# Two units that take turns, weights in three groups of blocks, and a plain first product in the last layers

## The chip, the cores and the metric

The kernel runs on one core of a Trainium2 chip. Five engines of the core work beside each other, each through its own queue in order: TensorE (PE, matmuls; its weight loads are PEld), VectorE (DVE), ScalarE (ACT), GpSimd (POOL) and SyncE (SP, which issues DMAs). The metric is the device time of one execution in microseconds; lower is better.

## The reference

Attention feeds a layer of eight experts, and that feeds one dense feed-forward layer. For 2 batches of 576 tokens, 8 heads of 64:

```
scores = q k^T / 8 + min(-(cum_i - cum_j), 0), causal;  attn = softmax(scores) v
x      = attn as 1152 tokens x 512
P      = exp(x w_gate - max), then 8 rounds of row and column normalisation
out    = sum over e of P[:, e] * (relu(x w1[e]) w2[e])       # w1: 512x1024, w2: 1024x512, 8 experts
y      = softplus(out w_in) w_out                            # w_in: 512x2048, w_out: 2048x512
```

All of it is float32; the last layer's weights come as 64-bit floats and are turned into float32 on the chip.

## The kernel before

Attention takes the first 118 us. After it the program runs 20 layers of one shape, numbered x = 0 to 19: each takes a 512x512 piece of a first weight and a 512x512 piece of a second one. Layers 0 to 15 are the experts' (NX = 16, two per expert; XE = 2 is the first layer of the second expert), layers 16 to 19 the dense layer's. Tokens are kept in two groups g of 576, each in two halves of 288 columns (HB).

Each float32 operand is held as two float32r parts, high and low, and a product is three matmuls: high by high, high by low, low by high.

The first product of a layer, x times w1, is done in Strassen's way with seven block products in place of eight. A `Unit` (x, p, g) makes two of the four 128-row blocks of the hidden layer, by the methods p1, p2, p6, p7, p5, p3, p4 in that order; each is six matmuls of 288 columns. p = 0 is unit a, p = 1 unit b, so that "a6" is p6 of unit a. The units share partial results within a PSUM bank: p1 leaves its product in bank `self.a`, ACT copies it out as `v` (L232, method `copy`), p6 adds its own product onto the same bank, ACT copies that as `u`, p5 adds again, and so on. So p6 may not start until the copy v is done, nor p5 until u is. DVE adds the copies to the other products (L245, L263, L274).

`evict` turns a finished block into the second product's operand `hh` (high) and `hl` (low). In layers 0 to 15 this is a ReLU: ACT L184, DVE L185. In layers 16 to 19 it is a softplus: ACT takes abs, exp and ln (L191 to L193), DVE L197 and L198, POOL L199 and L200 (which writes hh), DVE L203 and L204 (which writes hl). `defer` puts such pieces off by some flushes, and `flush` runs at each product and at each quarter of a second product.

`downs` is the second product: for each of nine tiles of 128 tokens, four quarters ("d") of three matmuls of 512 columns, in two PSUM banks y1 and y2 that alternate; DVE then adds the sum to `acc` (L296, L299).

The weights are prepared one layer ahead. `prep1` splits a w1 piece of one unit and makes four sums of its blocks: ACT L124 and DVE L128 for three raw blocks at once, POOL L125, L126, L129, L130 for the sums, then ACT L134 and DVE L136 for the four sums at once. `prep2` does the second weight (ACT L147, DVE and POOL L150). `convert` turns the 64-bit weights into float32 (L783 to L799, 32 pieces) from layer 2 on; `gate_steps` works out P during layers 0 and 1; `turn` transposes the experts' output for the dense layer; `build` makes the Strassen sums of x.

The order of all this is written by hand, as strings: `play` takes one product or one "d" after the other, and after each "d" the function `quarter` moves the background generators (`back`, `gates`, `conv`) on by one step. Within a layer the strings are, for the second group of tokens and then for the next layer's first group:

```
play("a1 a2", u) ... play("a6 a7 a5", u)
play("b1 d b2 d a3 d a4 d", u, d)              # then prep1(x + 1, 0) starts
play("b6 d b7 d b5 d d b3 d b4 d d d d d d d", u, d)
play("d d d d", {}, d)                         # prep1(x + 1, 1) has just started
play("a1 d a2 d a6 d d a7 d a5 d", u, d)
play("b1 d b2 d a3 d a4 d b6 d b7 d b5 d d b3 d b4 d", u, d)
```

Of the kernel before, what the change touches and what calls it, by code (L numbers as in the profile page):

```python
# [20 lines left out]
def attention_moe_ffn(ctx, tc, q, k, v, s, w_gate, w1, w2, w_in, w_out, out):  # L21
# [40 lines left out]
    A11, A12, A22, S1, S2, S3, S4 = range(7)  # L62
# [4 lines left out]
    def build(g, c, xr, xt_pool, quick):  # L67

        sub = nc.vector if quick else nc.gpsimd
        h, l = xh[g], xl[g]  # L70
        x1, x2 = xr[:, c, :], xr[:, c + 2, :]
        o = h[:, B11, c, :]
        nc.scalar.activation(out=o, in_=x1[:, :HB], func=AF.Copy)
        nc.vector.tensor_tensor(out=l[:, B11, c, :], in0=x1[:, :HB], in1=f(o), op=ALU.subtract)
        yield
        xt = xt_pool.tile([P, 4, HB], F32, tag="xt", name="xt", bufs=1)
        sub.tensor_tensor(out=xt[:, 0, :], in0=x1[:, HB:], in1=x1[:, :HB], op=ALU.subtract)
        yield
        o = h[:, B21:B22 + 1, c, :]
        z = x2.rearrange("p (j n) -> p j n", j=2)  # L80
        nc.scalar.activation(out=o, in_=z, func=AF.Copy)
        nc.gpsimd.tensor_tensor(out=xt[:, 2, :], in0=x2[:, HB:], in1=x1[:, HB:], op=ALU.subtract)
        sub.tensor_tensor(out=xt[:, 1, :], in0=x2[:, HB:], in1=xt[:, 0, :], op=ALU.subtract)
        yield
        nc.vector.tensor_tensor(out=l[:, B21:B22 + 1, c, :], in0=z, in1=f(o), op=ALU.subtract)
        sub.tensor_tensor(out=xt[:, 3, :], in0=x2[:, :HB], in1=xt[:, 1, :], op=ALU.subtract)
        yield
        o = h[:, T1:T4 + 1, c, :]
        nc.scalar.activation(out=o, in_=xt, func=AF.Copy)
        yield  # L90
        nc.vector.tensor_tensor(out=l[:, T1:T4 + 1, c, :], in0=xt, in1=f(o), op=ALU.subtract)
        yield
# [8 lines left out]
    order = [(x, which, i) for x in range(NH) for which in (1, 2) for i in range(2)]  # L101
    nxt = [0]

    def load_next():
        if nxt[0] >= len(order):
            return
        x, which, i = key = order[nxt[0]]
        nxt[0] += 1
        t = raw_p.tile([P, WQ], F32, tag="raw", name="raw")
        src = (w1 if which == 1 else w2)[x, i] if x < NX else wd[which][(x - NX) * 2 + i]  # L110
        nc.sync.dma_start(out=t, in_=src)
        raw_t[key] = t

    def prep1(x, p):

        if x >= NH:
            return
        t = raw_t.pop((x, 1, p))
        hi = w_p.tile([P, 7, HW], F32R, tag="w1h", name="w1h")
        lo = w_p.tile([P, 7, HW], F32R, tag="w1l", name="w1l")  # L120
        s4 = ws_p.tile([P, 4, HW], F32, tag="ws", name="ws")
        wt[(x, 1, p)] = (hi, lo)
        t = t.rearrange("p (b n) -> p b n", b=4)
        nc.scalar.activation(out=hi[:, :S1], in_=t[:, 1:], func=AF.Copy)  # L124
        nc.gpsimd.tensor_tensor(out=s4[:, 0, :], in0=t[:, 0, :], in1=t[:, 3, :], op=ALU.add)  # L125
        nc.gpsimd.tensor_tensor(out=s4[:, 1, :], in0=s4[:, 0, :], in1=t[:, 1, :], op=ALU.subtract)  # L126
        yield
        nc.vector.tensor_tensor(out=lo[:, :S1], in0=t[:, 1:], in1=f(hi[:, :S1]), op=ALU.subtract)  # L128
        nc.gpsimd.tensor_tensor(out=s4[:, 2, :], in0=t[:, 1, :], in1=t[:, 0, :], op=ALU.subtract)  # L129
        nc.gpsimd.tensor_tensor(out=s4[:, 3, :], in0=t[:, 2, :], in1=s4[:, 1, :], op=ALU.subtract)  # L130
        load_next()
        yield
        yield
        nc.scalar.activation(out=hi[:, S1:], in_=s4, func=AF.Copy)  # L134
        yield
        nc.vector.tensor_tensor(out=lo[:, S1:], in0=s4, in1=f(hi[:, S1:]), op=ALU.subtract)  # L136
        yield

    def prep2(x, i):
        if x >= NH:  # L140
            return
        t = raw_t.pop((x, 2, i))
        hi = w2_p[0].tile([P, 2, DM], F32R, tag=f"w2h{i}", name=f"w2h{i}", bufs=1)
        lo = w2_p[0].tile([P, 2, DM], F32R, tag=f"w2l{i}", name=f"w2l{i}", bufs=1)
        wt[(x, 2, i)] = (hi, lo)
        t = t.rearrange("p (c n) -> p c n", c=2)
        nc.scalar.activation(out=hi, in_=t, func=AF.Copy)  # L147
        yield
        for c in range(2):
            (nc.gpsimd if i else nc.vector).tensor_tensor(out=lo[:, c], in0=t[:, c], in1=f(hi[:, c]), op=ALU.subtract)  # L150
        load_next()
        yield
# [25 lines left out]
    lag = [0, 1]  # L178

    def evict(x, z, q, cols):  # L180

        hh, hl = hb[0][:, q, cols], hb[1][:, q, cols]
        if x < NX:
            nc.scalar.activation(out=hh, in_=z, func=AF.Relu)  # L184
            nc.vector.scalar_tensor_tensor(out=hl, in0=z, scalar=0.0, in1=f(hh), op0=ALU.max, op1=ALU.subtract)  # L185
# [9 lines left out]
        def sums():  # L195

            nc.vector.tensor_scalar(a2, a1, 1.0, -1.0, ALU.add, ALU.add)  # L197
# [797 lines left out]
```

## Time and profile before

| | |
|---|---|
| median of 3 runs | 1245.52 us (1243.07 to 1245.73) |
| the profiled execution | 1244.63 us, its span 1242.9 us |
| busy share of the span | PE 90%, PEld 78%, DVE 68%, ACT 42%, POOL 36% |
| instructions | 17931 |

The profiled execution's time is 1.7 us above its span, which counts from the first to the last instruction. A busy PE isn't PE at its peak: matmuls overlap, and what one costs is read from the distance of two starts. The idle time behind a row, in brackets, names what ended it.

### The profile page before, as it was taken

To read this page: it belongs to the slowest core of one execution; us is meant where nothing else is said; L and a number is where in the kernel's file an instruction comes from. 1 tells how busy PE (TensorE), PEld (TensorE's weight loads), DVE (VectorE), ACT (ScalarE), POOL (GpSimd) and SP (SyncE) were. 2 spreads that over 40 slices of the span, in tenths; PEclk is the share of its full clock that TensorE was granted. 3 is DMA by queue.
4 is the path that set the end of the run, shared out by engine and by line. 5 is a ranking of instruction groups with operands and counts; after the bars stand their busy time and mean duration, and the time that the engine had idled before them with its cause. 6 is when DMAs were issued, how large, how long until landed. Compare 5 with 4: busy or idle time off the path is not lost.

```text
span 1242.9 us, 17931 instructions
## 1 busy us (share of the span) xinstructions
PE 1113.2 (90%) x6596; PEld 963.3 (78%) x6596; DVE 850.4 (68%) x1703; ACT 520.4 (42%) x1138; POOL 450.4 (36%) x529
## 2 busy tenths in 40 slices
PE   6998998998999999999999999999999488796867
PEld 4766987888788888888888888898897467675766
DVE  4554437476878878778787787854556866676763
ACT  5987433232333433334334233332344545434441
POOL 8884102022432223323232232320212555546451
PEclk9989999899999999999999999999999789898999
DMA  5310101021322223222222132110110000101001
GB/s 172 99 59 14 52 17 51 17 96 58 119 85 86 82 75 107 86 85 94 76 95 101 69 102 80 66 60 17 69 51 17 35 18 17 51 18 38 14 9 68
DMA packets 30424, 78.48 MB, mean 63 GB/s; under 512 B 6048, under 2 KB 10656, under 8 KB 30336
## 3 DMA queue, kind: packets, MB, share of 16 engines
q1 hardware_dynamic: 27768, 68.93, 16.3%
q0 software_dynamic: 2560, 8.39, 1.7%
q8 instruction: 52, 0.85, 0.3%
q14 instruction: 36, 0.29, 0.1%
q10 hardware_dynamic: 8, 0.01, 0.0%
HBM read 66.02 MB, written 10.82 MB: 62 GB/s over the span
## 4 chain that ended last, share of the span: by engine, by line
PE 42%; DVE 28%; POOL 10%; ACT 9%; issue 9%; DMA 1%; SPq 1%; DVEq 0%; POOLq 0%; ACTq 0%
PE py L289 19%; PE ph L224 17%; DVE hl L185 3%; ACT hh L184 3%; DVE a L203 2%; DVE hl L204 2%; DVE acc L299 2%; DVE w2l L150 2%; POOL hh L200 2%; PE sc L462 2%; DVE ph L274 1%; DVE w1l L136 1%; DVE a L198 1%; POOL a L199 1%; POOL cm L798 1%
## 5 line engine op out<-in xcount | busy, mean ns | idle before, releaser
L224 PE MATMUL ph<-xh,w1h 128*128 128x288 f32 x1120 | 344.3, 307 | 89.5 <-ACT u L232 44.5
L224 PE MATMUL ph<-xh,w1l 128*128 128x288 f32 x1120 | 337.2, 301 | 0.0
L224 PE MATMUL ph<-xl,w1h 128*128 128x288 f32 x1120 | 336.7, 301 | 0.0
L224 PEld LDWEIGHTS ph<-xh,w1h 128*128 128x128 f32 x1120 | 216.2, 193 | 126.1 <-ACT u L232 52.5
L289 PE MATMUL py<-w2h,hh 128*128 128x512 f32 x720 | 292.2, 406 | 11.7 <-DVE acc L296 9.4
L289 PE MATMUL py<-w2h,hl 128*128 128x512 f32 x720 | 291.1, 404 | 1.2 <-DVE hl L204 1.2
L289 PE MATMUL py<-w2l,hh 128*128 128x512 f32 x720 | 291.2, 404 | 0.0
L224 PEld LDWEIGHTS ph<-xl,w1h 128*128 128x128 f32 x1120 | 217.2, 194 | 18.7
L224 PEld LDWEIGHTS ph<-xh,w1l 128*128 128x128 f32 x1120 | 217.0, 194 | 0.0
L798 POOL TENSOR_TENSOR cm<-cm,ct 128x512 f32<-128x512 f32 x32 | 42.4, 1324 | 365.4 <-DVE ct L797 365.4
L184 ACT ACTIVATE hh<-ph 128x288 fp32r<-128x288 f32 x192 | 78.3, 409 | 218.6 <-DVE ph L274 112.2
L289 PEld LDWEIGHTS py<-w2h,hl 128*128 128x128 f32 x720 | 138.7, 193 | 35.3 <-DVE hl L204 1.6
L289 PEld LDWEIGHTS py<-w2h,hh 128*128 128x128 f32 x720 | 140.2, 195 | 28.1 <-POOL a L199 10.6
L289 PEld LDWEIGHTS py<-w2l,hh 128*128 128x128 f32 x720 | 139.8, 194 | 13.3
L185 DVE SCALAR_TENSOR_TENSOR hl<-ph,hh 128x288 fp32r<-128x288 f32 x192 | 86.8, 455 | 62.0 <-ACT hh L184 60.2
L232 ACT ACTIVATE u<-ph 128x288 f32<-128x288 f32 x160 | 65.3, 408 | 141.7 <-PE ph L224 141.5
L299 DVE SCALAR_TENSOR_TENSOR acc<-py,gate,acc 128x512 f32<-128x512 f32 x126 | 93.6, 743 | 36.5 <-PE py L289 36.5
L150 POOL TENSOR_TENSOR w2l<-raw,w2h 128x512 fp32r<-128x512 f32 x40 | 53.1, 1347 | 165.6 <-ACT w2h L147 165.4
L199 POOL TENSOR_TENSOR a<-a,a 128x288 f32<-128x288 f32 x64 | 52.0, 813 | 108.2 <-DVE a L197 108.2
L134 ACT ACTIVATE w1h<-ws 128x1024 fp32r<-128x1024 f32 x40 | 42.1, 1051 | 73.1 <-POOL ws L130 73.1
L185 DVE SCALAR_TENSOR_TENSOR hl<-t,hh 128x288 fp32r<-128x288 f32 x64 | 43.3, 677 | 32.7 <-ACT hh L184 32.7
L203 DVE TENSOR_TENSOR a<-a,hh 128x288 f32<-128x288 f32 x64 | 38.4, 601 | 39.7 <-POOL hh L200 39.7
(177 smaller groups left out, 1598.6 us busy)
## 6 DMA issues: line engine op xcount, KB each, us to landing
raw<-in_w SPq DMA_DIRECT2D x64, 512.0 KB
f<-in_w_in SPq DMA_DIRECT2D x16, 512.0 KB
f<-in_w_out SPq DMA_DIRECT2D x16, 512.0 KB
wd<-cm POOLq DMA_DIRECT2D x32, 256.0 KB, 2.7
raw<-wd SPq DMA_DIRECT2D x16, 512.0 KB
out<-acc SPq DMA_DIRECT2D x9, 256.0 KB
vv<-in_v SPq DMA_DIRECT2D x8, 256.0 KB
qk<-in_k SPq DMA_DIRECT2D x7, 288.0 KB
```

Source lines behind the costliest of these rows:

```text
L134: nc.scalar.activation(out=hi[:, S1:], in_=s4, func=AF.Copy)
L150: (nc.gpsimd if i else nc.vector).tensor_tensor(out=lo[:, c], in0=t[:, c], in1=f(hi[:, c]), op=ALU.subtract)
L184: nc.scalar.activation(out=hh, in_=z, func=AF.Relu)
L185: nc.vector.scalar_tensor_tensor(out=hl, in0=z, scalar=0.0, in1=f(hh), op0=ALU.max, op1=ALU.subtract)
L199: nc.gpsimd.tensor_tensor(out=a2, in0=a1, in1=a2, op=ALU.subtract)
L200: nc.gpsimd.tensor_tensor(out=hh, in0=a3, in1=a2, op=ALU.add)
L203: nc.vector.tensor_tensor(out=a3, in0=a3, in1=f(hh), op=ALU.subtract)
L224: nc.tensor.matmul(o, u, v, start=(start and c == 0 and n == 0), stop=(c == 1 and n == 2), skip_group_check=True)
L232: nc.scalar.activation(out=t, in_=self.a, func=AF.Copy)
L289: nc.tensor.matmul(py, u, v, start=(k == 0 and n == 0), stop=(k == NF - 1 and n == 2))
L299: nc.vector.scalar_tensor_tensor(out=a, in0=py, scalar=gate_t[0][:, t, e:e + 1], in1=a, op0=ALU.mult, op1=ALU.add)
L798: nc.gpsimd.tensor_tensor(out=m, in0=m, in1=f(t), op=ALU.add)
```

## The change

It has these parts.

1. The two units take turns product by product: "a1 b1 a2 b2 a6 b6 ..." in place of five products of a, then two of b and so on. The strings are new (`A_SEQ`, `B_SEQ`), and the first group's products of layer 0 run ahead of the loop.
2. A w1 piece's seven blocks lie in three groups of 2, 2 and 3 blocks with tiles of their own, in place of one tile. `prep1` takes a group (0, 1, 2) for both units, and starts where the last product that reads the old group is past: "=0", "=1", "=2" in the strings. The four sums are made in place, in the raw tile, in two generators; a split is one group of ACT and DVE steps.
3. The second weight is prepared in quarters (`prep2(x, ft)`, "w0" to "w3") at the end of the layer before, in place of halves at the layer's start.
4. In layers 16 to 19 the first product is plain (`plain`): eight products of twelve matmuls for each group of tokens, no copies, no DVE adds. `turn` writes hh and hl of x directly, without `build`.
5. `evict` is put off in smaller pieces; in the softplus the second sum goes from POOL to DVE, and the high part is an ACT copy.
6. `downs` takes tiles 0 and 1, and 7 and 8, in pairs; a flush and a background step (`step`) follow each product and each quarter. The gate moves every sixth step, the conversion every third one and in seven steps a piece in place of four.

```
-        hi = w_p.tile([P, 7, HW], F32R, tag="w1h", name="w1h")
-        lo = w_p.tile([P, 7, HW], F32R, tag="w1l", name="w1l")
...
+        nb = (2, 2, 3)[g]
+        hi = w_p.tile([P, nb, HW], F32R, tag=f"w1h{g}", name=f"w1h{g}")
+        lo = w_p.tile([P, nb, HW], F32R, tag=f"w1l{g}", name=f"w1l{g}")
+        wt[x, 1, p, g] = (hi, lo)
+        for o, src in parts:
+            nc.scalar.activation(out=hi[:, o], in_=t[:, src], func=AF.Copy)
+            yield
+            yield
+            nc.vector.tensor_tensor(out=lo[:, o], in0=t[:, src], in1=f(hi[:, o]), op=ALU.subtract)
+            yield
...
             nc.vector.tensor_scalar(a2, a1, 1.0, -1.0, ALU.add, ALU.add)
+            nc.gpsimd.tensor_tensor(out=a2, in0=a1, in1=a2, op=ALU.subtract)
             nc.vector.scalar_tensor_tensor(out=a3, in0=z, scalar=0.0, in1=a3, op0=ALU.max, op1=ALU.add)
-            nc.gpsimd.tensor_tensor(out=a2, in0=a1, in1=a2, op=ALU.subtract)
-            nc.gpsimd.tensor_tensor(out=hh, in0=a3, in1=a2, op=ALU.add)
+
+        def high():
+            nc.vector.tensor_tensor(out=a3, in0=a3, in1=a2, op=ALU.add)
+            nc.scalar.activation(out=hh, in_=a3, func=AF.Copy)
 
         def rest_():
-            nc.vector.tensor_tensor(out=a3, in0=a3, in1=f(hh), op=ALU.subtract)
-            nc.vector.tensor_tensor(out=hl, in0=a3, in1=a2, op=ALU.add)
-
-        defer(lag[0], sums)
-        defer(lag[1], rest_)
+            nc.vector.tensor_tensor(out=hl, in0=a3, in1=f(hh), op=ALU.subtract)
+
+        defer(0, sums)
+        defer(2, high)
+        defer(3, rest_)
...
+    def plain(x, p, g, i, j):
+
+        o = ps.tile([P, 512], F32, tag="sc", name="ph", bufs=4)[:, :HB]
+        wh, wl = wt[x, 1, p, i]
+        ops = []
+        for r in range(2):
+            for c in range(2):
+                k = slice(c * P, (c + 1) * P)
+                h, l = xh[g][:, 2 * r + c, j, :], xl[g][:, 2 * r + c, j, :]
+                ops += [(wh[:, r, k], h), (wh[:, r, k], l), (wl[:, r, k], h)]
+        for n, (u, v) in enumerate(ops):
+            nc.tensor.matmul(o, u, v, start=(n == 0), stop=(n == 11))
+            if n == 5:
+                flush()
+                yield
+        flush()
+        evict(x, 0, o, p + 2 * i, slice(g * S + j * HB, g * S + (j + 1) * HB))
+        yield
...
+        A_SEQ = "a1 b1 a2 b2 =0 d d a6 d d b6 d d a7 d d b7 =1 d a5 d b5 d a3 d b3 d a4 d b4 d d"
+        B_SEQ = ("d d =2 a1 d d b1 d a2 d b2 d a6 d b6 d a7 d b7 d a5 d b5 d d w0 a3 d d w2 b3 d d w1 a4 d d w3 b4")
+        A_PLAIN = "p p p p d d p d p d p d p d =0 p d p d p d p d p d p d p d p =1 d d d"
+        B_PLAIN = "d d =2 d d p p d p d p d p p d p d p d p d p d p d d w0 p d d w2 p d d w1 p d d w3 p p"
+        A_GROUPS = [(0, 1), (2,), (3,)]
+        B_GROUPS = [(4,), (5,), (6,), (7, 8)]
```

How the order of the instructions moves, at two places. The first is ACT where the next layer's first products begin, in a layer that also converts weights: u and v are the copies that p6 and p5 wait for, w1h the split weights, cm the conversion. Before:

```order
L784 ACTIVATE cm<-f_5314 128x512
L124 ACTIVATE w1h<-raw 128x768
L134 ACTIVATE w1h<-ws 128x1024
L232 ACTIVATE v_5580<-ph 128x288
L184 ACTIVATE hh<-ph 128x288
L232 ACTIVATE u_5608<-ph 128x288
```

And in the change:

```order
L294 ACTIVATE v<-ph 128x288
L145 ACTIVATE w1h_5253<-raw_4813 128x256
L294 ACTIVATE v<-ph 128x288
L145 ACTIVATE w1h_5253<-raw_4813 128x512
L234 ACTIVATE hh<-ph 128x288
L145 ACTIVATE w1h_5298<-raw_4865 128x256
L871 ACTIVATE cm<-f_5128 128x512
L234 ACTIVATE hh<-ph 128x288
L294 ACTIVATE u<-ph 128x288
```

The copies v of both units now stand ahead of the weights' pieces, which are smaller, and three other instructions at most stand between a copy and the next one.

The second place is DVE in one of the layers 16 to 19; hl is the low part that ends an eviction, acc the sum of a second product. Before:

```order
L197 TENSOR_SCALAR a_11103<-a_11102 128x288
L198 SCALAR_TENSOR_TENSOR a_11104<-ph,a_11104 128x288
L197 TENSOR_SCALAR a_11125<-a_11124 128x288
L198 SCALAR_TENSOR_TENSOR a_11126<-ph,a_11126 128x288
L274 TENSOR_TENSOR ph<-ph,u_11033 128x288
L203 TENSOR_TENSOR a_11104<-a_11104,hh 128x288
L204 TENSOR_TENSOR hl<-a_11104,a_11103 128x288
L203 TENSOR_TENSOR a_11126<-a_11126,hh 128x288
L204 TENSOR_TENSOR hl<-a_11126,a_11125 128x288
```

And in the change:

```order
L257 SCALAR_TENSOR_TENSOR a_11049<-ph,a_11049 128x288
L260 TENSOR_TENSOR a_11049<-a_11049,a_11048 128x288
L383 TENSOR_TENSOR acc<-py,acc 128x512
L264 TENSOR_TENSOR hl<-a_11049,hh 128x288
L148 TENSOR_TENSOR w1l_11067<-raw_10648,w1h_11066 128x512
L255 TENSOR_SCALAR a_11083<-a_11082 128x288
L257 SCALAR_TENSOR_TENSOR a_11084<-ph,a_11084 128x288
L383 TENSOR_TENSOR acc<-py,acc 128x512
L260 TENSOR_TENSOR a_11084<-a_11084,a_11083 128x288
```

The adds that Strassen needs (L274 and the like) are gone, the four DVE steps of one eviction stand one eviction behind the other, and other work stands between them.

## Rows read from the trace of the kernel before

**Rows 1.** Page, part 2: PE's busy tenths in 40 slices of the span.

```profile
PE   6998998998999999999999999999999488796867
```

**Rows 2.** Windows by stage: length, busy us (instructions) of each engine, PE clock, DMA share, GB/s.

```profile
466.65:517.49 50.84, 48.10 (x267) 42.37 (x266) 39.43 (x66) 17.27 (x36) 14.74 (x15) 0.97 0.24 80
872.20:919.75 47.55, 47.55 (x279) 42.59 (x277) 24.90 (x44) 16.81 (x35) 8.46 (x11) 1.00 0.13 45
954.10:1060.40 106.30, 76.37 (x416) 67.01 (x417) 79.03 (x142) 58.72 (x126) 54.71 (x62) 0.88 0.07 25
1127.90:1196.60 68.70, 54.40 (x277) 46.16 (x277) 48.76 (x91) 29.97 (x67) 36.87 (x43) 0.92 0.06 21
```

**Rows 3.** Groups by line: out<-in, shapes, count | busy us, mean ns | idle before.

```profile
L224 PE MATMUL ph<-xh,w1h 128*128 128x288 f32 x1120 | 344.3, 307 | 89.5 <-ACT u L232 44.5 <-ACT v L232 37.2 <-DVE t L263 7.5
...
L289 PE MATMUL py<-w2h,hh 128*128 128x512 f32 x720 | 292.2, 406 | 11.7 <-DVE acc L296 9.4 <-ACT acc L294 2.3
...
L299 DVE SCALAR_TENSOR_TENSOR acc<-py,gate,acc 128x512 f32<-128x512 f32 x126 | 93.6, 743 | 36.5 <-PE py L289 36.5
...
L134 ACT ACTIVATE w1h<-ws 128x1024 fp32r<-128x1024 f32 x40 | 42.1, 1051 | 73.1 <-POOL ws L130 73.1
...
L124 ACT ACTIVATE w1h<-raw 128x768 fp32r<-128x768 f32 x40 | 33.6, 840 | 2.4 <-DMA raw<-in_w 2.4
...
L720 PE MATMUL pg<-xh,wgs 128*16 128x288 f32 x20 | 5.4, 294 | 0.0
```

**Rows 4.** Timeline of PE, layer 14's first quarter: start us, length us, instruction.

```profile
872.08 0.29 PE L224 MATMUL ph<-xh,w1l 128*128 128x288 f32 x1
872.21 0.39 PE L289 MATMUL py<-w2h,hh 128*128 128x512 f32 x1
872.44 0.39 PE L289 MATMUL py<-w2l,hh 128*128 128x512 f32 x1
```

**Rows 5.** Timeline of PE, its two waits in the steady stretch.

```profile
414.12 0.40 PE L224 MATMUL ph<-xh,w1h 128*128 128x288 f32 x1 [0.43 <-ACT u L232]
...
441.66 0.40 PE L224 MATMUL ph<-xh,w1h 128*128 128x288 f32 x1 [2.28 <-ACT v L232]
```

**Rows 6.** Timeline of ACT ahead of PE's wait at 441.66.

```profile
434.36 0.83 ACT L124 ACTIVATE w1h<-raw 128x768 fp32r<-128x768 f32 x1
440.25 1.06 ACT L134 ACTIVATE w1h<-ws 128x1024 fp32r<-128x1024 f32 x1 [5.06 <-POOL ws L130]
441.21 0.39 ACT L232 ACTIVATE v<-ph 128x288 f32<-128x288 f32 x1
```

**Rows 7.** Timeline of ACT and PE, start of layer 0.

```profile
121.55 1.16 ACT L89 ACTIVATE xh<-xt 128x1152 fp32r<-128x1152 f32 x1 [2.29 <-DVE xt L86]
...
124.01 0.61 PE L224 MATMUL ph<-xh,w1h 128*128 128x288 f32 x1 [4.16 <-ACT v L232]
```

**Rows 8.** Timeline of PE, layer 16.

```profile
981.40 0.61 PE L224 MATMUL ph<-xh,w1h 128*128 128x288 f32 x1 [11.41 <-ACT u L232]
```

**Rows 9.** Timeline, softplus evictions in layers 16 and 17, and 18.

```profile
1010.19 0.73 POOL L125 TENSOR_TENSOR ws<-raw 128x256 f32<-128x256 f32 x1
1010.27 0.97 DVE L203 TENSOR_TENSOR a<-a,hh 128x288 f32<-128x288 f32 x1 [1.43 <-POOL hh L200]
...
1131.12 0.46 DVE L203 TENSOR_TENSOR a<-a,hh 128x288 f32<-128x288 f32 x1 [3.22 <-POOL hh L200]
...
1135.66 0.41 ACT L191 ACTIVATE a<-ph 128x288 f32<-128x288 f32 x1 [5.98 <-DVE ph L245]
1136.10 0.45 ACT L192 ACTIVATE a<-a 128x288 f32<-128x288 f32 x1
1136.58 0.31 DVE L197 TENSOR_SCALAR a<-a 128x288 f32<-128x288 f32 x1 [1.01 <-ACT a L192]
1136.97 0.80 POOL L199 TENSOR_TENSOR a<-a,a 128x288 f32<-128x288 f32 x1 [2.76 <-DVE a L197]
```

**Rows 10.** Timeline, the last matmul.

```profile
1238.43 0.40 PE L289 MATMUL py<-w2h,hl 128*128 128x512 f32 x1
```

More of the change, by code (lines that the diff above doesn't have):

```diff
@@ L100, in attention_moe_ffn, with load @@
     w2_p = []
[L101 to L114, printed above, removed]
+    def load(x, which, i):
@@ new lines, in load, with split @@
+        raw_t[x, which, i] = t
+    def split(x, p, g, parts, engine=None):
+        t = raw_t[x, 1, p]
+        nb = (2, 2, 3)[g]
[8 more added lines that the diff above has]
+            yield
@@ L141, in prep2 @@
             return
[L142 to L147, printed above, removed]
+        if g == 0:
+            if x < NX:
+                for p in range(2):
+                    yield from sums1(x, p)
+            for p in range(2):
+                yield from split(x, p, 0, [(slice(0, 2), slice(2, 4))])
+            if x < NX:
+                for p in range(2):
+                    yield from sums2(x, p)
+        elif g == 1:
+            for p in range(2):
+                yield from split(x, p, 1, [(slice(0, 2), slice(1, 3) if x < NX else slice(1, 5, 3))])
+                if x >= NX:
+                    load(x + 1, 1, p)
+        elif x < NX:
+            for p in range(2):
+                yield from split(x, p, 2, [(slice(0, 1), slice(0, 1)), (slice(1, 3), slice(3, 5))])
+                load(x + 1, 1, p)
@@ new lines, in downs @@
+    def downs(x, groups):
+        for tiles in groups:
+            py = {}
+            for t in tiles:
+                nd[0] += 1
+                py[t] = ps.tile([P, DM], F32, tag=f"y{1 + nd[0] % 2}", name="py", bufs=1)
+            for k, ft in enumerate((0, 2, 1, 3)):
+                wh, wl = wt[x, 2, ft]
+                for t in tiles:
+                    tsl = slice(t * P, (t + 1) * P)
+                    hh, hl = hb[0][:, ft, tsl], hb[1][:, ft, tsl]
+                    for n, (u, v) in enumerate(((hh, wh), (hh, wl), (hl, wh))):
+                        nc.tensor.matmul(py[t], u, v, start=(k == 0 and n == 0), stop=(k == NF - 1 and n == 2))
+                    flush()
+                    if k == NF - 1:
+                        total(x, t, py[t])
+                    yield
@@ L468, in attention_moe_ffn @@
             split_ends(0)
-            load(4)
-            load(5)
-            for n in range(3):
-                load_next()
+            load_qk(4)
+            load_qk(5)
+            for which in (1, 2):
+                for i in range(2):
+                    load(0, which, i)
             scores(units[0])
@@ L826, in attention_moe_ffn, with step @@
         gates = gate_steps()
-        conv = convert(cv_p)
+        conv = iter(())
         back = []
-        nstep = [0]
-        def bg(k=1):
-            for _ in range(k):
-                while back and next(back[0], 1):
-                    back.pop(0)
+        tick = [0]
+        def step():
+            tick[0] += 1
+            if x < XE:
+                if tick[0] % 6 == 0:
+                    next(gates, None)
+            elif x < NX - 2 and tick[0] % 3 == 0:
+                next(conv, None)
+            while back and next(back[0], 1):
+                back.pop(0)
@@ L935, in attention_moe_ffn @@
                 gt.close()
-                for t in range(NTT):
-                    z = acc[0][:, t, :]
-                    nc.vector.tensor_scalar(z, z, gate[:, t, 0:1], None, ALU.mult)
+                conv = convert(cv.enter_context(tc.tile_pool(name="cv", bufs=2, reuse_waits="tile")))
         drain()
```

342 lines of the change are left out of this document (174 added, 168 removed).

## The prediction

> **What bounds the kernel now.** I read the slices first, then windows, groups, timelines. The slices [rows 1] show PE busy nine tenths and more from slice 11 to slice 31, then holes: the trouble seems to lie in the last quarter, layers 16 to 19. But matmuls overlap, so a busy PE may still be waiting; the windows tell it apart. Layer 14, from first quarter to first quarter of the next, takes 47.55 us with PE busy throughout at full clock; layer 6, with the same matmuls, takes 50.84, and layer 18 takes 68.70 [rows 2]. So 47.55 is what a layer costs when PE waits for nobody. That fits the starts [rows 4]: a 288-column matmul is followed after 0.13 us, one of 512 columns after 0.23. A layer has 3 x 1120 / 20 = 168 of the first and 3 x 720 / 20 = 108 of the second [rows 3]; with 0.1325 and 0.2335 they make 47.5 us.
>
> No other engine is near its limit in layer 6: DVE 39.4 of 50.8 us, ACT 17.3, POOL 14.7 [rows 2]. PE waits because queues run in order. The groups say for whom: of the 89.5 us that PE idled ahead of the first product's matmuls, 81.7 ended with ACT's copies u and v [rows 3]. The steady layers have two such waits, 2.28 us for v and 0.43 for u [rows 5]; the difference to 47.55 is 3.29, so each costs some 0.3 us more than its idle time. Ahead of the v at 441.21 ACT sat on L134, which waited 5.06 us for POOL's sums [rows 6]: the copy was ready to run and stood in line. At layer 0's start it is the same with L89, the sums of x, and costs 4.16 us [rows 7]. In layers 16 to 19 the softplus makes the queues longer and PE waits up to 11.41 us [rows 8].
>
> **The change, part by part**, on the profiled span of 1242.9 us.
>
> *Up to the first product at 118.0 us.* Attention is untouched but for w1's splits for layer 0: eight ACT instructions in place of four. From 840 ns for 768 columns and 1051 for 1024 [rows 3], an ACTIVATE costs 207 ns and 0.82 ns a column, so four more cost 0.8 us. It is nothing if other work hides it and can't be a gain; ACT's exponentials stand in every step of attention, so I take all of it: 118.8.
>
> *From 118.0 to the end of layer 15's second product, at 954.1: 836.1 us.* Bare work is 16 x 47.55 = 760.8, and the gate's own matmuls some 6.5 (40 of 288 columns [rows 3] at 0.13, and a few small ones). So 68.8 us are lost to waits and to the low clock after them. What the change does to each:
> - Copies. With a and b in turn, three products of 0.79 us (6 x 0.1325) and two quarters of 0.70 (3 x 0.2335) stand between a1 and a6, 3.8 us in place of one product and at most two quarters. The copy takes 0.39 [rows 6], and ACT's row order now has it ahead of small weight pieces (512 columns: 0.63 us). POOL's sums start some 12 steps, 9 us, before ACT's pieces read them. I cost both steady waits at nothing; their cover is 3.8 us against copy and one piece, 1.0 us, so ACT may be 2.8 us late before it shows.
> - Weights. w1 and w2 splits need eight more ACT instructions and four more DVE ones a layer: 1.7 us of ACT and under 1 of DVE, beside PE. PE reads the last group about five steps after its split.
> - DVE. Its work for a layer stays at some 40.2 us, but in 47.55 instead of 50.84: 85% busy. Tightest is PSUM: tile 2 takes the bank of tile 0 one quarter and one product (1.49 us) after tile 0 ended, and the sum in between (L299) takes 0.74 on DVE [rows 3]. Tile 8 follows tile 6 likewise. So DVE may lag 0.75 us there. I take 0.3 us a layer.
> - Layer 0's start: the sums come before the splits now and save about 1.5 us of the chain; PE has four products in hand (3.2 us) in place of two. Of 4.16 us and the slow matmuls behind it about 1 stays.
> - The gate moves every sixth step, 4.4 us, against as little as 2.1 where quarters stood alone; I keep 4 us of its losses, and 2 for the first load of the conversion.
>
> Residue 1 + 4 + 2 + 14 x 0.3 = 11. New length 760.8 + 6.5 + 11 = 778.3, a gain of 57.8.
>
> *From 954.1 to the last matmul's end at 1238.8 [rows 10]: 284.7 us.* The plain product has 24 more matmuls of 288 columns a layer, 3.2 us: 50.7 bare, 202.8 for four. That is the price, and it is certain. It buys: twelve copies and twelve DVE adds a layer fewer, and nothing in PE waits for ACT within a product. What can be late next is the eviction. Its loop, in the order in which ACT stands, is abs 0.41, exp 0.45, DVE 0.31, POOL 0.80, DVE 0.46, copy 0.45 (as exp) [rows 9] and six hand-overs of 0.03 to 0.08: 3.1 us, since the next abs stands behind the copy. PE makes such a block in two halves and two quarters, 2.99 us, in most of the string, 1.58 where halves stand alone (there two evictions overlap), 4.4 near a layer's end. So the loop lags by up to about 2 us and catches up where quarters stand together; four banks allow more than that. I take 1.3 us a layer. DVE has 48.8 - 12 x 0.46 = 43 us of work in 50.7.
>
> The turn: some 40 transposes, 4 us. Behind them PE runs twenty halves with hardly a quarter between, 21 us, while DVE has ten evictions (each 0.31 and three of 0.46 to 0.97, about 2.0) and the turn's own low parts, about 25. I keep 7 us, with the low clock. Sum: 202.8 + 5.2 + 4 + 7 = 219.0, a gain of 65.7.
>
> *The tail* is 4.1 us; tiles 7 and 8 now end 0.7 us apart and share the way out: 4.4.
>
> 118.8 + 778.3 + 219.0 + 4.4 = 1120.5 span, and with the 1.7 above it 1122.2. The profiled run lies 0.9 below the median of before, so I say **1123 us**.
>
> **Rivals.**
>
> *DVE takes PE's place.* At 85% an in-order queue with waits in it may be full. For: DVE's adds of two SBUF operands stretch beside POOL, L203 0.97 us against 0.46 [rows 9], and more POOL work stands behind fewer idle microseconds. Against: layer 14, without conversion, ran with no wait at all, and layer 6 leaves DVE idle for 11 us. Price: half of the steady wait stays in eleven layers (1.65 x 11 = 18), and the evictions carry the nine sums of 0.74 in their loop (16 x 3.13 + 6.7 = 56.8, 4.8 more than I took, x 4 = 19): 1159. The Trainium skill, "SBUF — State Buffer", section "Who interferes with whom", states that such a DVE instruction contends with a GpSimd one that reads SBUF, and that the first one issued holds the shared pair for its whole length. The stretched L203 agrees; by that rule the sixteen L199 left would cost DVE up to 13 us a layer, which makes 56 for a dense layer too. That the change takes as many POOL adds away is why I don't follow it.
>
> *Nothing is left over.* The residues go (11 to 2, 7 to 3, 5.2 to 0): 1104. For: layer 14. Against: the gate is a true chain between PE and DVE.
>
> *Slower: the raw weights come late.* A raw w1 tile is now loaded only when the last group of the layer before has been split, with two buffers in place of three shared ones. From there to the first sum are some 25 steps, 19 us. Each microsecond that a load takes beyond that is paid in each of fourteen layers and more; it outweighs the gain of 122 from 28 us a load on, and loads of 29 us would end at 1122 + 14 x 10 = 1262. Against: DMA is busy 24% in layer 6 at 80 GB/s [rows 2], and there 512 KB at that rate take 6.6 us.
>
> *It doesn't do what it says*: PE's waits were DVE's all along and move with them. That is the first rival at full size (3.3 x 11 = 36 more, dense layers at 60, 8 x 4 = 32 more): 1190.
>
> **How the numbers follow.** Forecast 0.59, nothing left 0.12, DVE 0.19, full-size DVE 0.05, slower 0.03, 0.02 for no change. The range from 1104 to 1165 leaves out the last three and a little of the first two's ends. A difference below 0.2%, 2.5 us, can't be told from none; all cases but the slow one lie far below: faster 0.95, same 0.02, slower 0.03.
>
> **What would show it.** In the changed profile: layers 3 to 15 47.6 to 48.0 us apart with no wait for u or v over 0.3 us; dense layers 51 to 53 apart; PE's clock near 1.00 from layer 3 on; DVE at about 85% of a converting layer; one stretch of some 7 us of idle PE at the turn. I am wrong if converting layers take over 49 us, with PE waiting for DVE's sums (acc) or for a PSUM bank; if dense layers take over 55, with PE waiting for acc, hh or hl; or if POOL's first sums or ACT's split wait for a DMA.

## The result, and the profile after

The changed kernel took 1129.45 us (median of four runs, 1127.72 to 1131.76) beside 1244.3 for the kernel before on the same chip: a ratio of 0.9081, 95% interval 0.9056 to 0.9107. I had said 1123, range 1104 to 1165. The profiled run took 1129.13 us, its span is 1127.4.

The page of the kernel after: busy tenths of PE and DVE and PE's clock in 40 slices, and the two groups of PE that answer to L289 and L224 [rows 1, 3]:

```profile
PE   5989899999999999999999999999999999999998
DVE  4555537749878787787787777864555576666664
PEclk8998999999999999999999999999999999999999
...
L371 PE MATMUL py<-w2h,hh 128*128 128x512 f32 x720 | 287.2, 399 | 10.7 <-DVE acc L383 6.3
...
L286 PE MATMUL ph<-xh,w1h 128*128 128x288 f32 x896 | 265.9, 297 | 0.4 <-ACT v L294 0.3
```

The 89.5 us that PE idled ahead of a product's first matmul are 0.4, and 0.8 in the plain product (L350). What is left stands ahead of the quarters, mostly for DVE's adds into acc.

Windows of the kernel after, as in [rows 2] (length, then busy us of PE, PEld, DVE, ACT and POOL): layers 6 and 14 (from first quarter to first quarter), the turn, layer 18:

```profile
443.66:491.14 47.48, 47.48 (x279) 42.56 (x278) 37.72 (x73) 18.59 (x44) 15.91 (x17) 1.00 0.29 97
823.50:870.98 47.48, 47.48 (x279) 42.56 (x278) 24.25 (x47) 17.48 (x41) 6.74 (x8) 1.00 0.15 44
910.00:928.05 18.05, 16.12 (x117) 14.74 (x116) 16.45 (x34) 14.14 (x34) 6.88 (x8) 1.00 0.18 59
1032.55:1086.40 53.85, 51.09 (x302) 45.66 (x301) 35.94 (x80) 30.66 (x73) 15.52 (x19) 1.00 0.03 11
```

Layer 6, with conversion, now takes exactly what layer 14 takes without, and so do all from 4 to 14: they are bare, that is, without waits. Layer 18 lost 14.9 us against before although PE has more to do in it.

Three stretches are not bare. In attention, from 84 us on, PE does less and then its clock falls; windows of the kernel before first, then of the one after:

```profile
84.00:88.00 4.00, 3.40 (x39) 2.53 (x39) 2.99 (x19) 3.58 (x10) 3.19 (x6) 1.00 0.04 12
88.00:92.00 4.00, 4.00 (x40) 3.02 (x38) 2.08 (x12) 4.00 (x14) 2.49 (x4) 1.00 0.32 86
```

```profile
84.00:88.00 4.00, 2.23 (x27) 1.58 (x27) 3.96 (x20) 2.31 (x7) 3.07 (x5) 0.98 0.00 0
88.00:92.00 4.00, 3.89 (x21) 3.03 (x22) 1.97 (x10) 3.17 (x11) 2.36 (x4) 0.50 0.31 86
```

From 87.9 to 94.7 us PE's clock is at 0.50. At 80 us the two kernels are level, at 97 the one after is some 4 us behind, and its first product starts at 122.26, not 118.0. (The kernel before has such a fall too, from 69.1 to 75.9.) Layers 0 to 3 take 52.5, 54.2, 51.0 and 49.1 us. Waits of PE between 122 and 349 us (total, times, longest), and below them DVE's stand at the conversion's first load:

```profile
PE py L371 <- DVE acc L388: 3.4, 2, 2.5
PE pcs L830 <- DVE hl L237: 3.1, 1, 3.1
PE pg L807 <- DVE hl L237: 1.0, 1, 1.0
```

```profile
253.65 0.43 DVE L870 TENSOR_SCALAR f<-f 128x512 f32<-128x512 f32 x1 [5.96 <-DMA f<-in_w_in]
```

In the dense layers (51.6, 52.9 and 53.9 apart) PE waits for acc, 5.8 us in five places. ACT's queue there shows a loop:

```profile
1060.37 0.45 ACT L251 ACTIVATE a<-a 128x288 f32<-128x288 f32 x1
1062.16 0.45 ACT L261 ACTIVATE hh<-a 128x288 fp32r<-128x288 f32 x1 [1.34 <-DVE a L260]
1062.51 0.39 ACT L249 ACTIVATE a<-ph 128x288 f32<-128x288 f32 x1
...
1065.20 0.44 ACT L261 ACTIVATE hh<-a 128x288 fp32r<-128x288 f32 x1 [1.34 <-DVE a L260]
1065.55 0.39 ACT L249 ACTIVATE a<-ph 128x288 f32<-128x288 f32 x1
```

From one copy hh to the next it takes 3.04 us; the next block's abs (L249) starts only behind the copy, which waits 1.34 us for DVE.

### The profile page after: what moved, and what is told of

Read it like the earlier page. It is cut to its first block, busy times and chain, and to the rows that moved or that the text cites. A ratio compares the mean times of both kernels' runs of the same rounds, so it can differ in the third digit from the quotient of the medians.

```text
span 1127.4 us, 18117 instructions
## 1 busy us (share of the span) xinstructions
PE 1085.5 (96%) x6692; PEld 952.9 (85%) x6692; DVE 750.0 (67%) x1705; ACT 525.8 (47%) x1246; POOL 358.7 (32%) x429
## 4 chain that ended last, share of the span: by engine, by line
PE 80%; DVE 8%; ACT 5%; issue 3%; POOL 3%; DMA 1%; SPq 0%; POOLq 0%; ACTq 0%; DVEq 0%
PE py L371 40%; PE ph L286 30%; PE ph L350 3%; PE sc L550 2%; POOL a L256 1%; DVE a L260 1%; PE pv L662 1%; ACT a L250 1%; ACT a L249 1%; PE tr L636 1%; DVE a L255 1%; ACT eb L605 1%; DVE acc L383 1%; PE tr L630 1%; DVE a L257 1%
## 5 line engine op out<-in xcount | busy, mean ns | idle before, releaser
L371 PE MATMUL py<-w2h,hl 128*128 128x512 f32 x720 | 285.0, 396 | 0.0
L371 PE MATMUL py<-w2l,hh 128*128 128x512 f32 x720 | 284.9, 396 | 0.0
L286 PE MATMUL ph<-xh,w1l 128*128 128x288 f32 x896 | 265.6, 296 | 0.0
L286 PE MATMUL ph<-xl,w1h 128*128 128x288 f32 x896 | 264.2, 295 | 0.0
L286 PEld LDWEIGHTS ph<-xh,w1h 128*128 128x128 f32 x896 | 168.9, 188 | 18.3 <-ACT v L294 1.5
L286 PEld LDWEIGHTS ph<-xl,w1h 128*128 128x128 f32 x896 | 169.2, 189 | 16.6
L286 PEld LDWEIGHTS ph<-xh,w1l 128*128 128x128 f32 x896 | 169.1, 189 | 0.0
L294 ACT ACTIVATE v<-ph 128x288 f32<-128x288 f32 x128 | 50.9, 411 | 168.7 <-PE ph L286 160.4
L148 DVE TENSOR_TENSOR w1l<-raw,w1h 128x512 fp32r<-128x512 f32 (+1 forms) x144 | 94.3, 655 | 9.8 <-ACT w1h L145 9.5
L145 ACT ACTIVATE w1h<-raw 128x512 fp32r<-128x512 f32 (+1 forms) x144 | 83.0, 576 | 1.6 <-PE ph L286 1.6
L350 PE MATMUL ph<-xh,w1h 128*128 128x288 f32 x256 | 76.0, 297 | 0.8 <-ACT xh L912 0.8
```

What stands on the lines that cost most here:

```text
L145: nc.scalar.activation(out=hi[:, o], in_=t[:, src], func=AF.Copy)
L148: nc.vector.tensor_tensor(out=lo[:, o], in0=t[:, src], in1=f(hi[:, o]), op=ALU.subtract)
L286: nc.tensor.matmul(o, u, v, start=(start and c == 0 and n == 0), stop=(c == 1 and n == 2), skip_group_check=True)
L294: nc.scalar.activation(out=t, in_=self.a, func=AF.Copy)
L350: nc.tensor.matmul(o, u, v, start=(n == 0), stop=(n == 11))
L371: nc.tensor.matmul(py[t], u, v, start=(k == 0 and n == 0), stop=(k == NF - 1 and n == 2))
```

## The experiments

In the diffs, - is the changed kernel. Layers are given by the distance of their first quarters.

**The cover undone**, for unit a. One product stands between a1 and a6, and between a6 and a5:

```diff
- A_SEQ = "a1 b1 a2 b2 =0 d d a6 d d b6 d d a7 d d b7 =1 d a5 d b5 ..."
- B_SEQ = ("d d =2 a1 d d b1 d a2 d b2 d a6 d b6 d a7 d b7 d a5 d b5 ...")
+ A_SEQ = "b1 b2 a1 a2 =0 a6 a7 a5 d d d d b6 d d b7 d d d =1 b5 d d a3 ..."
+ B_SEQ = ("d d =2 b1 d d b2 d d a1 a2 a6 a7 a5 d d d d b6 d b7 d b5 ...")
```

> The changed kernel (1129.5 us) with one part undone: the order of the products in layers 0 to 15 is put back to one in which a single product (0.79 us) stands between a1 and a6 and between a6 and a5, whose bank ACT's copies v and u must have left. The weights stay in three groups, POOL's sums spread over the steps. Theory (what made the copies late was ACT standing on a weight split that waited for POOL; with sums a dozen steps ahead ACT is free, and 0.79 us covers a copy of 0.39): 1129 to 1136, PE waiting for u and v together under 10 us, the layers 5 to 15 at 47.5 to 48.0. Rival (the longer cover of 3.8 us is what took the waits away): the layers back at 50 to 50.8, 1160 to 1175, PE waiting for u and v by over 30 us.

1163.18 us, ratio 0.9358 (0.9331 to 0.9384): 33.7 more than the changed kernel. Layers 4 to 11 take 49.4 to 50.9 us, 12 to 14, where little or no conversion is left, 48.4. Layers 0 to 3 lose 16 of the 33.7 us. Waits of PE from 260 to 860 us, and ACT ahead of two waits:

```profile
PE ph L286 <- ACT v L294: 15.3, 12, 3.8
PE ph L286 <- ACT u L294: 1.6, 3, 0.7
```

```profile
511.47 0.41 ACT L234 ACTIVATE hh<-ph 128x288 fp32r<-128x288 f32 x1 [0.64 <-DVE ph L307]
511.77 0.41 ACT L294 ACTIVATE v<-ph 128x288 f32<-128x288 f32 x1
```

```profile
254.83 0.68 ACT L871 ACTIVATE cm<-f 128x512 f32<-128x512 f32 x1 [7.08 <-DVE f L870]
255.41 0.40 ACT L234 ACTIVATE hh<-ph 128x288 fp32r<-128x288 f32 x1
255.71 0.41 ACT L294 ACTIVATE v<-ph 128x288 f32<-128x288 f32 x1
```

My theory fell and the rival held: even with the sums made early a copy is late behind 0.79 us. At 511.77 it stands behind the eviction of the product before, which stands on DVE's sum; at 255.71, ahead of PE's longest wait (7.14 us), behind the conversion's first piece as well.

This is not the old wait come back. The kernel before waited 2.28 us for v in the next layer's first group ([rows 5], 441.66), where two quarters stood between as well; here the waits for v lie in the second group, 2.5 to 5 us ahead of a layer's first quarter. The 33.7 us are what the cover is worth in this order, not against the order of before.

**The early sums undone**, in layers 1 to 15, with the order in turns kept:

```diff
-            if x < NX:
+            if x == 0:
                 for p in range(2):
                     yield from sums1(x, p)
...
-            if x < NX:
+            if x == 0:
                 for p in range(2):
                     yield from sums2(x, p)
         elif g == 1:
             for p in range(2):
+                if 0 < x < NX:
+                    for _ in sums1(x, p):
+                        pass
+                    for _ in sums2(x, p):
+                        pass
...
```

> The changed kernel (1129.5 us) with another part undone: from layer 1 on the four POOL sums of each weight piece are issued in one go directly ahead of the ACT split that reads them, as before the change, so that ACT stands on POOL for some 5 us. The order in turns stays. Theory (ACT's standing is what made PE wait, but the cover of 3.8 us takes most of it up): 1129 to 1140, a wait of PE on a copy of 0 to 1 us a layer. Rival 1 (only the early sums matter, cover or not): the steady waits of 3.3 us a layer are back, 1160 to 1175. Rival 2 (none of it matters, since PE waited for DVE all along): within 2 us of 1129.5, and so for the next kernel.

1137.35 us, 0.9153 (0.9126 to 0.9180): 7.9 more. ACT in layer 5 and in layer 6 (449.0 to 496.5 us):

```profile
412.34 0.63 ACT L145 ACTIVATE w1h<-raw 128x512 fp32r<-128x512 f32 x1 [8.48 <-POOL raw L161]
...
459.01 0.63 ACT L145 ACTIVATE w1h<-raw 128x512 fp32r<-128x512 f32 x1 [5.00 <-POOL raw L161]
459.55 0.41 ACT L299 ACTIVATE v<-ph 128x288 f32<-128x288 f32 x1
```

The 5.00 is as long as the 5.06 of [rows 6], yet this layer takes 47.48 us: nothing of it reaches PE. But the v behind it is another copy, that of p5 (method `p5`), which p3 waits for with one product and two quarters between (2.2 us); it ends at 459.96, and a3 starts at 459.99. Behind the 8.48 in layer 5 PE waited 1.83 us for such a v. That layer is longer by 2.7 us, and layer 2, where the conversion starts, by 3.4. The time is the theory's; that the cover of 3.8 us takes the stall up isn't shown, since no stall stood ahead of a copy with that cover.

**Both undone** (the two edits together).

> Both parts undone together: short cover of 0.79 us, and POOL's four sums directly ahead of ACT's split. Theory (either of the two is enough to hide the copies, and without both the old wait is back): layers 3 to 15 at 50 to 51.5, PE waiting for u and v by 2 to 4 us a layer, 1160 to 1180. Rival (it was the shorter weight pieces, 512 columns in place of 768 and 1024, or the size of the steps that took the waits away): 1129 to 1140.

1166.73 us, 0.9385 (0.9363 to 0.9407), 37.3 more, layers 4 to 11 at 48.9 to 50.4, 0.5 to 2 us under the 50.84 of [rows 2]. Waits of ACT's split for POOL from 350 to 860 us, in the kernel before, with the early sums undone, and here:

```profile
ACT w1h L134 <- POOL ws L130: 47.2, 10, 5.1
```

```profile
ACT w1h L145 <- POOL raw L161: 26.8, 11, 8.5
```

```profile
ACT w1h L145 <- POOL raw L161: 0.8, 3, 0.5
```

In this order ACT hardly stands on POOL, so the old stall and the short cover never met, and the run is little else than the first experiment again (3.6 us more). Whether either is enough against that stall stays open. Early sums alone don't make the copies free, as the first experiment's order shows, where they stand behind other things. What took away the old 2.28 us is not isolated: the cover, the early sums, the smaller pieces and the new places of the splits all changed there, and the last two were not tried by themselves.

**Short cover, copy first.** The order of the first experiment, and in p1, p6 and p5 the copy ahead of the deferred evictions:

```diff
             self.product(self.a, A11, B11, True)
+            self.v1 = self.copy("v")
             flush()
-            self.v1 = self.copy("v")
...
```

> The first experiment's order with one product of 0.79 us as cover (1163.2 us), and one exchange: the copies u and v are issued on ACT ahead of the deferred eviction steps of the products before, not behind them. In the first experiment the v of 511.77 stood behind the hh of 511.47, which had waited 0.64 us for DVE's sum. Theory (with a short cover the copy is late because it stands behind an eviction's hh that waits for DVE): most of the waits for v and u between 260 and 860 us (16.9 us) go, layers 5 to 15 at 47.5 to 48.2, 1136 to 1146. Rival (it stands behind the weight pieces, or the sums on DVE behind it are late in any order): 1158 to 1166.

1145.99 us, 0.9211 (0.9182 to 0.9239). Layers 4 to 14 take 47.9 to 49.3 us. Waits of PE from 260 to 860 us:

```profile
PE ph L286 <- ACT v L294: 3.4, 3, 2.5
PE py L371 <- DVE acc L388: 2.9, 11, 1.3
PE ph L286 <- ACT u L294: 0.4, 1, 0.4
```

From 16.9 to 3.8 us: most copies there had stood behind evictions. Half of what the cover is worth, 17 of 33.7 us, is to be had by ACT's order alone. The wait behind the conversion's first piece stays (5.2 us at 253.4).

**POOL's second sum in the softplus, as before:**

```diff
-        def high():
-            nc.vector.tensor_tensor(out=a3, in0=a3, in1=a2, op=ALU.add)
-            nc.scalar.activation(out=hh, in_=a3, func=AF.Copy)
+            nc.gpsimd.tensor_tensor(out=hh, in0=a3, in1=a2, op=ALU.add)
 
         def rest_():
-            nc.vector.tensor_tensor(out=hl, in0=a3, in1=f(hh), op=ALU.subtract)
+            nc.vector.tensor_tensor(out=a3, in0=a3, in1=f(hh), op=ALU.subtract)
+            nc.vector.tensor_tensor(out=hl, in0=a3, in1=a2, op=ALU.add)
...
-        defer(2, high)
         defer(3, rest_)
```

> The changed kernel with the softplus eviction of the dense layers as before: POOL writes hh with the second sum, DVE takes two adds for hl, ACT makes no copy; sums at the next step, the rest three steps on. In the changed kernel ACT's abs of a block stands behind the copy of the block before, a loop of 3.04 to 3.18 us in layer 18, and PE waits there 13.9 us in all for acc and the weights' load behind it. Theory (that loop through ACT is what the dense layers lose): without the copy the dense layers go from 51.6 to 53.9 apart down to 51 to 51.5, 1121 to 1126. Rival (what they lose is DVE, which stretches beside POOL): 16 more POOL sums and 16 more DVE adds a layer make them 54 to 58, 1138 to 1150.

1127.77 us, 0.9073 (0.9051 to 0.9095): no difference. DVE's two adds in this kernel from 930 to 1125 us:

```profile
L261 DVE TENSOR_TENSOR a<-a,hh 128x288 f32<-128x288 f32 x58 | 35.3, 608 | 47.9 <-POOL hh L258 47.9
L262 DVE TENSOR_TENSOR hl<-a,a 128x288 fp32r<-128x288 f32 x58 | 32.0, 551 | 2.2
```

The dense layers are 50.7, 52.6 and 52.8, a little shorter, the turn is 1.7 longer. Neither theory: the eviction's form doesn't matter much either way. (PE itself waits 5.8 us for acc in the changed kernel; the 13.9 in the expectation count the 8.1 of its weight loads too, which overlap.)

**The eviction's last steps later:**

```diff
-        defer(2, high)
-        defer(3, rest_)
+        defer(4, high)
+        defer(5, rest_)
```

> The changed kernel with the last two steps of a softplus eviction two quarter steps later (four and five in place of two and three), so that ACT's abs and exp of the next block stand ahead of the copy of this one. It takes away the loop in which the abs of the next block waits for the copy (3.04 us a block in layer 19 of the changed kernel). Theory (that loop is what PE waits for in the dense layers): these come 50.8 to 51.5 apart in place of 51.6, 52.9 and 53.9, PE waits for acc under 2 us in all, 1123 to 1126. Rival (the acc adds are late because DVE does its steps in order behind the eviction's, whichever of its own are in flight): no change, 1128 to 1131, or later by what the low part now costs at a layer's end, up to 1135.

1120.23 us, 0.9015 (0.8993 to 0.9037): 9.2 less, the layers 51.0, 51.3 and 51.3, the turn 2.2 shorter. PE's waits from 915 us on, this kernel:

```profile
PE py L371 <- DVE acc L383: 0.8, 2, 0.4
PE ph L350 <- DVE xl L914: 0.7, 1, 0.7
```

The theory of the loop held, with a larger gain than I had worked out (3.5 to 6.5).

**The acc add first**, in layers 15 to 19:

```diff
+                    if k == NF - 1 and x >= NX - 1:
+                        total(x, t, py[t])
                     flush()
-                    if k == NF - 1:
+                    if k == NF - 1 and x < NX - 1:
                         total(x, t, py[t])
```

> The changed kernel with one exchange in layers 15 to 19: when a tile's last quarter is done, DVE's add into acc is issued ahead of the eviction's deferred steps, not behind them. Theory (PE waits in the dense layers for a PSUM bank whose acc add stands on DVE behind steps that wait for ACT and POOL): the waits for acc (5.8 us in 5 places, up to 1.5) go, 1122 to 1126. Rival (the add then delays the eviction by its 0.68 us, and PE waits for hh and hl in its place): 1128 to 1131.

1124.47 us, 0.9048 (0.9029 to 0.9066); layers 51.6, 51.3, 52.2. This interval overlaps that of the changed kernel, but the waits for acc fell from 5.8 to 1.9 us: the theory held in the trace, as one of two ways to take away the same waits.

**Seven products in the dense layers too**, in turns, with copies and sums as in layers 0 to 15:

```diff
...
-            if x < NX:
+            if True:
                 u = dict(a=Unit(x, 0, g), b=Unit(x, 1, g))
...
```

> The changed kernel with the first product of the dense layers (16 to 19) in seven products and sums again, as before the change, in the order of turns of the other layers and with the new eviction. It issues 24 fewer 288-column matmuls a layer, and a dozen more copies on ACT and adds on DVE. At the turn x is built anew with its sums; two of the eviction's buffers have three copies in place of four. Theory (the plain product paid because DVE and not PE would set the pace): DVE has some 43 + 12 x 0.46 = 48.8 us of work a layer, with waits between, so the layers come 52 to 57 apart and the turn is longer, 1130 to 1150. Rival (with the units in turn nothing waits, so the plain product only costs its 3.2 us a layer): 48 to 50 apart, 1114 to 1121.

1202.43 us, 0.9675 (0.9648 to 0.9701): 73 more. Layers of 63.9, 68.9 and 69.0, as long as before the change; they make up 43 of the 73 us, the turn 19, the last layer 12. Window from layer 17's first quarter to layer 18's, three of PE's waits in it, and ACT and DVE during the longest:

```profile
1012.63:1081.50 68.87, 55.41 (x276) 47.41 (x277) 46.80 (x95) 37.40 (x89) 22.15 (x26) 0.85 0.11 31
```

```profile
1016.00 0.61 PE L284 MATMUL ph<-xh,w1h 128*128 128x288 f32 x1 [1.56 <-ACT v L292]
1027.42 0.50 PE L372 MATMUL py<-w2h,hh 128*128 128x512 f32 x1 [1.60 <-DVE acc L384]
1046.06 0.80 PE L372 MATMUL py<-w2h,hh 128*128 128x512 f32 x1 [6.96 <-ACT hh L259]
```

```profile
1041.36 0.41 ACT L247 ACTIVATE a<-ph 128x288 f32<-128x288 f32 x1 [1.46 <-DVE ph L337]
1042.28 0.31 DVE L253 TENSOR_SCALAR a<-a 128x288 f32<-128x288 f32 x1 [0.66 <-ACT a L248]
1044.31 0.41 ACT L247 ACTIVATE a<-ph 128x288 f32<-128x288 f32 x1 [1.25 <-DVE ph L337]
1045.23 0.31 DVE L253 TENSOR_SCALAR a<-a 128x288 f32<-128x288 f32 x1 [0.66 <-ACT a L248]
1045.58 0.43 ACT L259 ACTIVATE hh<-a 128x288 fp32r<-128x288 f32 x1
```

The direction was that of the theory, the size nearly four times the most that it gave, and its reason is wrong: DVE has 46.80 us of work in 68.87 and is not full. PE waits 14.3 us in all, 7 of them at one place, the first quarter behind the last products, for hh; and the granted clock, 0.85 on average, is at 0.50 for some 20 us. While PE stands, ACT and DVE wait for each other in turn: the abs of the next block (L247) for DVE's sum of p4 (L337), DVE's next step for ACT's exp, 2.95 us a block, and the hh that PE waits for stands behind the last of these. Six of a unit pair's eight half blocks become ready within its last six products. The plain product gives one every twelve matmuls, and has no such sum. That two of the eviction's buffers had three copies in place of four doesn't show: no wait of ACT's abs ends with the POOL sum that frees one.

**The same with the later steps**, as in the run that gained 9.2; at the turn, where these products stand without quarters between, two deferred steps are issued behind each:

```diff
-        defer(2, high)
-        defer(3, rest_)
+        defer(4, high)
+        defer(5, rest_)
...
-                play("a5 b5 a3 b3 a4 b4", u)
+                for z in "a5 b5 a3 b3 a4 b4".split():
+                    play(z, u)
+                    flush()
+                    flush()
```

> The seven products and sums in the dense layers (1202.4 us), now with the last two steps of the softplus eviction two quarter steps later, as in the run that took 9 us off the changed kernel. In that earlier run a dense layer held 55.41 us of PE, 46.80 of DVE and 37.25 of ACT in 68.87, so no engine was full. Theory (the loop of the eviction through ACT's copy is what made these layers 69 us long, and the plain product paid because it takes copies and sums out of this loop): 50 to 56 a layer, 1130 to 1155. Rival (the copies v and u and DVE's sums in the products are themselves the chain, whatever the eviction's last steps do): 64 to 70 a layer, 1185 to 1205.

1213.46 us, 0.9756 (0.9733 to 0.9780): longer still, layers of 62.6 to 72.2, the wait for hh 9.13 at the longest.

```profile
1048.67 0.80 PE L372 MATMUL py<-w2h,hh 128*128 128x512 f32 x1 [9.13 <-ACT hh L259]
```

So the loop through the copy alone isn't what made them long; where a block's high part is what PE waits for, putting it later costs. The layers are about the rival's, the time lies above it. That the bunched evictions and DVE's sums between them are the cause fits both traces; neither was tried by itself.

**Layer 0's splits twice as fast in attention:**

```diff
                     next(prework, None)
+                    next(prework, None)
```

> The changed kernel with two steps of layer 0's weight splits at each step of attention in place of one, so that they end near 55 us of the span, as before the change, and not near 98. In the changed kernel DVE was busy 3.96 of 4 us between 84 and 88, PE 2.23, and its clock fell to 0.5 and 0.66 in the 8 us behind; the first product started at 122.3 in place of 118.0 before. Theory (the late splits made that hole): first product at 118 to 119.5, 1125.5 to 1127. Rival (it is the new order of the x build and of its four sums on POOL): first product at 121.5 to 123, 1128 to 1131.

1127.71 us, 0.9070 (0.9042 to 0.9097), the first product at 121.65: inconclusive by this trace. PE's clock fell between 84 and 92 us here too (0.70 on average). In the next run, whose attention is the same, it didn't. The runs' mean clocks say more: 1123.97 and 1125.67 us at 0.991 and 0.989, where the changed kernel took 1127.72 and 1129.76; the other two, 1129.76 and 1130.00, ran at 0.986. So at the same clock the edit may be worth some 4 us, an estimate from two pairs of runs.

**The good edits together**: later copy, acc first, faster splits.

> Three edits of the earlier runs together on the changed kernel: the last two steps of a softplus eviction later (1120.2 alone), DVE's acc add ahead of them in layers 15 to 19 (1124.5 alone), the weight splits of layer 0 in two steps at a time (1127.7 alone). If they add up to what each took off 1129.5, 1113.5. If the first two take away the same waits, as the theory of the loop has it (with the loop gone PE waited only 0.8 us for acc): 1117 to 1120.

1115.54 us, 0.8964 (0.8940 to 0.8988). That is between the two figures: beside the later copy alone, the dense layers take 1.8 us less in all and the first product starts 4.6 earlier. Dense layers 50.66, 50.58 and 50.64, the 50.7 bare that I had worked out for the plain product. The first product starts at 117.92; PE has no hole at 84 us, and the clock stayed up:

```profile
84.00:88.00 4.00, 3.41 (x41) 2.48 (x41) 2.90 (x19) 3.67 (x11) 3.29 (x6) 1.00 0.04 13
```

**And the gate moved** away from the second products:

```diff
-                if tick[0] % 6 == 0:
+                if (tick[0] - 14) % 64 in (10, 17, 24, 31, 47, 54, 61):
```

> The same three edits, and the gate's 18 steps no longer at every sixth step but at seven fixed places of a layer where neither of the two PSUM banks that it shares with the second products (a2, b2) is held by an eviction. In the changed kernel the gate's matmul waited 3.1 us there in layer 1 and 1.0 in layer 0. Theory (that is the loss of the layers 0 to 3 beside the start of the conversion): 4 to 6 us less than the kernel without it, layer 2 starting 50 us behind layer 1 in place of 54. Rival (the gate's own chain between PE and DVE is what costs, wherever it stands): within 2 us of it.

1108.46 us, 0.8907 (0.8882 to 0.8932), the fastest of all, 21 under the changed kernel. The gain is above the 4 to 6 expected (7.1), and the place another: layers 0 and 1 take 53 us as they did; from the first product to layer 0's first quarter 3.5 us go (1.6 of them twelve of the gate's matmuls, now behind that quarter), and layer 2, where the conversion starts, comes down from 52.6 to 47.9. DVE stands there 2.6 us for the first load, in place of 6.4 in the kernel without this edit, and PE's waits for acc are 0.9 in place of 3.8. At both places the clock of the kernel without this edit was at 0.50 for 3.4 us (118.4 to 121.8, 255.0 to 258.4) and here is not, so part of the 7.1 is clock.

## Why the prediction was right, point by point

The mechanism and the sign were right; the sum is 6.9 us short on the span: 3.5 in attention, 3.3 in the expert layers.

- *The copies at nothing* held: no wait for u or v is over 0.3 us. I gave two reasons, the cover of 3.8 us and POOL's early sums, and didn't weigh them. Cutting the cover to one product costs 33.7 us, issuing the sums late 7.9. Which of the two took away the old wait no run tells, since none has the old stall ahead of a copy of p1 or p6. What I had not in the argument is the eviction that stands ahead of a copy on ACT; in [rows 6] one sees the split alone. It is in the order shown with the change, though: five instructions, two of them evictions, stand between the second v and u there, not three at most.
- *0.3 us a layer for DVE and the PSUM bank*: nothing from layer 4 on. DVE has 37.72 us of work in a converting layer, 79%, not 40.2.
- *Attention, +0.8*: it was +4.2. I priced four ACT instructions and looked for no harm to PE. In the ten traces with the splits at this pace the first product starts at 121.15 to 124.19; in the three with the faster splits at 121.65, 117.92 and 118.98. So the late splits are the likely cause, with the clock's fall on top; what sets the clock off stays open.
- *Expert layers 778.3*: from 122.26 to layer 15's last quarter at 909.98 it is 787.7. Four halves of layer 16's first product (3.2) and the turn's first twenty transposes (2.85 of PE) fall into this stretch, which I counted behind it; without them it is 781.7. The rest are mis-sized waits. Up to layer 4 the kernel lost 22.2 us beside its bare work, where I had 17.5 for all layers: gate 6.5, waits 11. The gate's waits (1.0, 0.3 and 3.1) had the clock at 0.50 behind the longest. Layers 2 and 3, where the conversion starts, lost 3.6 and 1.6: I took 2 for its first load and looked at PE only, not at DVE's queue, where DVE stood 5.96 us. The 4.2 that I had for DVE came to nothing and hid half of this.
- *Dense layers 219.0*: with what stands ahead of 909.98 it is 219.3, and that is luck. The layers lost some 8.5 us in place of 5.2 (0.9 to 3.1 each), the transposes took 5.8 in place of 4, for which I had no row, and the turn lost about 3 in place of 7. The loop of 3.1 us is there with 3.04, at the place that I named; that four banks bear it was wrong: it delays DVE's acc add, and two banks hold py.
- *The plain product's price of 3.2 us a layer* held, as the 50.6 of the combined kernel shows. What it buys I named (copies and sums fewer) and left without a number: 73 us in all beside the rest of the change, the turn's 19 among them.
- *The first rival*, DVE in PE's place, fell. The Trainium skill, "SBUF — State Buffer", section "Who interferes with whom", has a DVE instruction with two SBUF inputs contend with a GpSimd one that reads SBUF. The trace agrees: with POOL's second sum back, the first of the two adds (L261) took 0.46 us each of the 43 times that no POOL instruction ran beside it, and 0.88 to 1.53 in 20 of the 21 others. That this would set a layer's time no run shows; two adds at 608 and 551 ns on average stand in layers that are the shorter ones.
- *Late raw weights* fell: POOL's first sums waited 1.6 us for a load in the whole run. *Nothing left over*, 1104, wasn't reached by this kernel; the last experiment comes to 1108 with the gate, the eviction and DVE's queue put right.

## What to carry to other kernels

When an engine waits for a short copy, read what stands ahead of the copy in its in-order queue: here one order put three products between, and with one in their place 33.7 us were lost, though ACT's split no longer stood on POOL. Check a cover against the longest thing that may stand in that queue, the eviction of the product before among them. When two parts are undone together, read in the trace whether both of the old waits are back: here the stall on POOL was not. And an algorithm with fewer matmuls, whose results come late, in a bunch and by way of other engines' sums, can lose to a plain one that gives them evenly: 24 more matmuls a layer bought 73 us.

## What the runs showed of the hardware

PE's granted clock fell to 0.50, the lower of its two levels (1.2 GHz), behind four microseconds in which PE was busy for 2.23. With 3.40 and 3.41 in the same place it stayed at 1.00, but in the last kernel, with 3.51, it fell within them (0.80 on average): their busy time doesn't settle it. The hole itself is 1.2 us (3.40 less 2.23). The 6.8 us at 0.50 behind it, from 87.9 to 94.7, cost up to 3.4 more, an estimate from half their length. And the same attention kept the clock in one kernel and lost it in another (first product at 117.92 and 121.65), so some 4 us of a comparison can hang on it.

A DVE add of two operands in SBUF (128x288) took 0.46 us with no POOL instruction beside it, and twice that and more with one: the second add (L262) of the kernel with POOL's sum 0.93 to 1.44 us in all 14 such cases, and at most 0.46 in the 50 others.

A load that DVE waited 6 us for was paid two queues on: DVE stood for it, its acc adds came late, and then PE's quarters did.
